# Delta-rule attention and two feed-forward layers: another order of the layers' passes, other constants in the planner, and GpSimd's arithmetic moved to VectorE

## The chip, the core and the metric

The kernel runs on one core of a Trainium2 chip. The core has a matrix engine (TensorE, PE in the profile; PEld is its weight load), a vector engine (VectorE, DVE), a scalar engine (ScalarE, ACT), GpSimd (POOL) and the SyncE queue (SP), which issues all transfers here. The metric is the device time of one execution in microseconds, as the median of several runs.

## What is computed

A delta-rule attention over 768 positions for 4 batches of 8 heads of width 48, then two feed-forward layers over the resulting 3072 rows of 384:

```python
for t in range(S):
    kt, vt, bt = (k_n[:, :, t], v[:, :, t], beta[:, :, t, None])
    y[:, :, t] = np.einsum('bhd,bhde->bhe', q[:, :, t], state)
    v_old = np.einsum('bhde,bhd->bhe', state, kt)
    state = state + bt[:, :, :, None] * np.einsum('bhd,bhe->bhde', kt, vt - v_old)
...
h = x @ w_in;  g = np.maximum(0.01 * h, h);  x = g @ w_out      # layer 0
h = x @ w_in;  g = h - np.tanh(h);           out = g @ w_out    # layer 1
```

Here `k_n` is `k` divided by its norm. Both layers have 2048 hidden features.

## The kernel before

**Numbers in two halves.** Every matmul operand is a pair of f16 tiles, a high part and the rest that it leaves, and a product is three matmuls. So each f32 result is split after it is made: ScalarE writes the high part, VectorE the rest. The weights arrive in 64-bit words and are made into f32 on VectorE (`w_f32`, one shift and two combining instructions for each piece), summed in squares for a scale, and split. There are four weights: 0 (`w1_in`), 1 (`w1_out`), 2 (`w2_in`), 3 (`w2_out`).

**Units and chunks.** The positions are cut into 12 chunks of 64; two chunks make a unit (6 units, 0 to 5). A chunk holds 4 x 64 = 256 rows for the feed-forward layers. For a unit, `keys` and `grams` make normalised keys and their products `gd` (L821, `g_batch` L803, which multiplies `gd` twice on GpSimd, L813 and L814), `inverses` (L832) solves 32x32 triangular systems in `xi` by 60 dependent multiplies and adds, 30 of each, and `merges` (L861) joins the blocks to 64x64 in `XF`. For each chunk then `queries`, `products` (L901, with a mask multiply on `pq`), `states`, `outputs` and `to_xa` make its 256 rows, `xa`. The states go from chunk to chunk.

**Which engine.** `inv_eng` (L858) puts the solve on VectorE in unit 0 and on GpSimd in units 1 to 5; `p_engs` (L914) puts the mask on VectorE for the first four chunks and on GpSimd after; the second half of `g` in layer 0 (L1041) and the zeroing of `XF` (L883) may go to either, as the planner chooses.

**Passes.** `layer(n, i)` (L1105) takes chunk n through layer i: eight times, `h_part` (L1021) makes 256 hidden features (18 matmuls of 256 columns, whose result ScalarE and VectorE turn into `g`), and `o_part` (L1046), three parts later, multiplies `g` with the second weight. The last part of layer 0 hands on to `to_xb`, which makes the input of layer 1. There are 24 passes. Before the change they go unit by unit (L1159): layer 0 of its two chunks, then layer 1 of the two.

**The order.** All work is first put into a graph (`Graph`). `tails` gives each node a priority, the length of the work behind it up to the end. `schedule` then plays the program through, with a cost for each instruction (`cost`), places in buffer rings (`room`), and a `lock` that keeps GpSimd's work and VectorE's two-input work apart, and writes each engine's instructions in the order in which they began there. On the chip each engine runs its own list in that order and waits by semaphores where an input is late. Since rings such as `g` and `ps_h` are handed out in the order of the program, the passes stand in TensorE's list in the order in which `layer` is called. Ring `x` has 6 places; `x_r.most["a"]` says how many of these may hold `xa`.

Of the kernel before, what the change touches and what calls it, by code (L numbers as in the profile page):

```python
# [18 lines left out]

KS = 64.0  # L20
POW2 = 0x7F800000


class Buf:
# [79 lines left out]
class Graph:  # L104


    LAT = dict(pe=0.16, act=0.033, dve=0.033, pool=0.08, sp=0.033)
    SPAN, WARM = 10.24 / 3, 3060.0
    ISSUE, DEEP, RATE = 0.47, 8, 370e3

    def __init__(self, nc):
        self.eng = dict(pe=nc.tensor, act=nc.scalar, dve=nc.vector, pool=nc.gpsimd, sp=nc.sync)
# [19 lines left out]
    def cost(self, eng, op, writes, reads, kw):  # L132
        n = max([v.free for v in writes[:1] + reads])
        wide = [v for v in reads if v.free > 1 or n == 1]
        psum = any(v.psum for v in writes + reads)
        pointer = n > 1 and any(v.free == 1 for v in reads)
        half = all(SIZE[v.ap.dtype] == 2 for v in writes + wide)
        if eng == "dve":
            rate = 0.96
            if op == "transpose":  # L140
                rate = 0.53
            elif op == "memset":
                rate = 1.54
            elif op == "reciprocal":
                rate = 0.16
            elif not psum and op in ("tensor_copy", "tensor_scalar"):
                rate = 3.84 if half and op == "tensor_copy" else 1.92
            elif not psum and op == "tensor_tensor" and half:
                rate = 1.92
            d = 0.15 + n / rate / 1e3 + (0.05 if pointer else 0.0) + (0.02 if psum else 0.0)  # L150
            if op == "memset":
                d = 0.06 + n / rate / 1e3
            two = op in ("tensor_tensor", "scalar_tensor_tensor") and sum(not v.psum for v in wide) > 1
            lock = two or (not psum and op in ("tensor_copy", "tensor_scalar") and n > 8)
            return d, d - 0.08, lock
        if eng == "act":
            d = 0.18 + n * 0.000833 + (0.09 if pointer else 0.0) + (0.1 if "accum_out" in kw else 0.0)
            return d, d - 0.1, False
        if eng == "pool":
            d = 0.12 + n * {"memset": 0.0008, "tensor_scalar": 0.001}.get(op, 0.00205)  # L160
            return d, d - 0.04, True
        return 0.0, self.ISSUE, False
# [3 lines left out]
    def depend(self, node, v, write, eng):  # L166
        psum = v.psum
        p0, p1, lo, hi = v.region()
        log = v.buf.log
        if v.buf.ring is not None and not log:  # L170
            node.new.append(v.buf)
        for q0, q1, l, h, m, w in log:
            if m is node:
                continue
            if psum or ((w or write) and p0 < q1 and q0 < p1 and lo < h and l < hi):
                node.preds.add(m)
        if write or psum:
            log[:] = [e for e in log if not (p0 <= e[0] and e[1] <= p1 and lo <= e[2] and e[3] <= hi)]
        log.append((p0, p1, lo, hi, node, write))
        if v.buf.ring is not None and v.buf not in node.bufs:  # L180
            node.bufs[v.buf] = True
            v.buf.users.append(node)

    def put(self, calls, writes, reads, dma=0):
        node = Node(len(self.nodes), calls)
        self.nodes.append(node)
        self.open = None
        for v in reads:
            self.depend(node, v, False, "")
        for v in writes:  # L190
            self.depend(node, v, True, "")
        node.cost = {e: self.cost(e, c[0], writes, reads, c[1]) for e, c in calls.items()}
        node.dma = dma
        return node

    def cut(self):
        self.open = None
# [59 lines left out]
    def schedule(self, prio):  # L257
        nodes = self.nodes
        need = [len(n.first) for n in nodes]
        ready = [0.0] * len(nodes)  # L260
        gone = [False] * len(nodes)
        self.start, self.end = [0.0] * len(nodes), [0.0] * len(nodes)
        engs = ("pe", "act", "dve", "pool", "sp")
# [1 line left out]
        heap = {e: ([], []) for e in engs}  # L265
        clock = dict.fromkeys(engs, 0.0)
        lock = dma = 0.0
        past, cols, lands = deque(), 0.0, []
        rings = {}
        left, head, held = {}, {}, {}  # L270
        for n in nodes:
# [19 lines left out]

        def offer(n, r):
            for i, e in enumerate(n.calls):
                heappush(soon[e], (max(r, ready[n.idx]) + self.LAT[e], prio[n.idx], n.idx, i))

        def again(r, t):
            queue = rings[r][1]
# [8 lines left out]
        while len(order) < len(nodes):  # L306
# [51 lines left out]
            if e == "pe":  # L358
                while past and past[0][0] < t - self.SPAN:
                    cols -= past.popleft()[1]  # L360
                if cols < self.WARM:
                    occ = n.cold
                    dur = occ + 0.2
                past.append((t + occ, n.cols))
                cols += n.cols
            if e == "sp":
# [6 lines left out]
            n.on = e  # L373
            clock[e] = t + occ
            if locked:
                lock = t + dur - (0.05 if e == "dve" else 0.0)
            self.start[i], self.end[i] = t, t + dur
            order.append(n)
# [15 lines left out]
                    again(b.ring, b.end + 0.03)  # L394
            for m in n.succs:
                need[m.idx] -= 1
                if e != "pe" or m.main != "pe":
                    ready[m.idx] = max(ready[m.idx], t + dur)
                else:
                    ready[m.idx] = max(ready[m.idx], t + occ - self.LAT["pe"])  # L400
                if not need[m.idx]:
                    offer(m, t)
            for m in n.after:
# [16 lines left out]
def kernel(  # L420
# [14 lines left out]
    NM = k.shape[3]  # L435
# [26 lines left out]
        return Ring(name, [t[:, 0:width] for t in ts], short, order)  # L462

    x_r = ring("x", 6, KT * N, order=False)
    x_r.most["a"] = 5
    s_r = ring("sx", 4, 512, short=True)
    g_r = ring("g", LAG + 1, 512)
    kf_r = ring("kf", 2, NM * D)
# [46 lines left out]
    def copy(o, i, scale=1.0):  # L515
        act(out=o, in_=i, func=ACTF.Copy, scale=scale)
# [6 lines left out]
    def tt(o, a, b, op, engs=("dve",)):  # L523
        either(engs, "tensor_tensor", out=o, in0=a, in1=b, op=op)
# [278 lines left out]
    def g_batch(n, g, Gd, bt):  # L803

        s, m0, kt = n % 2, g * GM, KTp[n % 3]
        ps = bank(C)
        for m in range(GM):
            k2 = [parts(kt, HS[h], m0 + m) for h in range(2)]
            heads([(ps[HS[h], m], k2[h], k2[h]) for h in range(2)])
        gv = slice(s * NM + m0, s * NM + m0 + GM)  # L810
        copy(Gd[:, gv], ps[:, :, 0:HB], maskb[:, 0:1])
        stt(Gd[:, gv], ps[:, :, HB:], maskb[:, 1:2], Gd[:, gv], ALU.mult, ALU.add)
        tt(Gd[:, gv], Gd[:, gv], tri.unsqueeze(1).to_broadcast([128, GM, HB]), ALU.mult, ("pool",))  # L813
        tt(Gd[:, gv], Gd[:, gv], bt[:, s * NM + m0:s * NM + m0 + GM].unsqueeze(2).to_broadcast([128, GM, HB]),  # L814
           ALU.mult, ("pool",))
        av = slice(gv.start + 1, gv.stop + 1)
        split(AT[:, 0, av], AT[:, 1, av], ps[:, :, HB:], half[:, 0:1])

# [37 lines left out]
        return nat  # L856

    def inv_eng(u):  # L858
        return "dve" if u == 0 else "pool"

    def merges(u, nat):  # L861

        def last2(t, r, m):
            return [t[r, m, :, c_] for c_ in range(2)]

        def bank2():
            t = g_.tile(ps_a, [128, 512], F32)
            g_.cut()
            return t[:, 0:NM * HB].rearrange("p (m n) -> p m n", m=NM)

        for i in range(2):
            m0 = i * NM
            pm = bank2()
            for m in range(NM):
                heads([(pm[HS[h], m], [AT[HS[h], c_, m0 + m:m0 + m + 2].rearrange("p m j -> p (m j)") for c_ in range(2)],
                        last2(nat, HS[h], m0 + m)) for h in range(2)])
            split(PM[:, 0, :, 0:HB], PM[:, 1, :, 0:HB], pm, half[:, 1:2])
            ps = bank2()
            for m in range(NM):
                heads([(ps[HS[h], m], parts(PM, HS[h], m), last2(TT, HS[h], m0 + m)) for h in range(2)])  # L880
            split(XH[:, m0:m0 + NM, :, 0], XH[:, m0:m0 + NM, :, 1], ps, -1.0 / KS)
            for h in range(2):
                memset(TWO, XW[HL[h], m0:m0 + NM, 0:HB], 0.0)  # L883

    q_t, qs_t, p_t = {}, {}, {}

# [25 lines left out]
            tt(pg, pg, maskp.unsqueeze(1).to_broadcast([128, 2 * GM, C]), ALU.mult, p_engs(n))  # L912

    def p_engs(n):  # L914
        return ("dve",) if n < 4 else ("pool",)

    def states(n):

# [102 lines left out]
    def h_part(i, x, p, kap):  # L1021
# [8 lines left out]
                node = mm(ps[:, j * N:(j + 1) * N], WI[i][:, 2 * p + j, 1 - a, t], x[b][:, t], n == 0, n == 3 * KT - 1)  # L1030
            g_.ffn(node)
        sx = g_.tile(s_r, [128, 2 * N], F32)
        if i == 0:
            act(out=sx, in_=ps, func=ACTF.Prelu, scale=C0, alpha=0.01)
        else:
            act(out=sx, in_=ps, func=ACTF.Tanh, scale=kap[:, 0:1])
            stt(sx, sx, kap[:, 1:2], ps, ALU.mult, ALU.add)
        g = g_.tile(g_r, [128, 2, 2 * N], F16)
        if i == 0:
            copy(g[:, 0], sx)  # L1040
            tt(g[:, 1], sx, g[:, 0], ALU.subtract, TWO)  # L1041
        else:
            split(g[:, 0], g[:, 1], sx, C0)
        return g
# [94 lines left out]
    for u in range(NU):  # L1139
# [9 lines left out]
        for s in range(2):  # L1149
# [6 lines left out]
            states(n)  # L1156
            outputs(n)
            to_xa(n)
    for u in range(NU):  # L1159
        for i in range(2):  # L1160
            for s in range(2):
                layer(2 * u + s, i)
    while pend:
        o_next()
    g_.prepare()
# [48 lines left out]
```

## Time and profile before

| what | value |
|---|---|
| median of 3 runs | 1098.94 us (1098.93 to 1102.3) |
| the profiled execution's own time | 1101.25 us |
| its span, first to last instruction | 1098.8 us |
| TensorE busy | 977.9 us (89%) |
| VectorE busy | 711.8 us (65%) |
| ScalarE busy | 647.4 us (59%) |
| GpSimd busy | 304.9 us (28%) |

The span is what the durations below are counted in; 2.45 us lie around it in the profiled execution. A busy share is an average over stretches that differ: the slices of the span show VectorE nearly full up to a quarter of the span, and TensorE from there on. Matmul ends are modelled, so a busy TensorE may still wait a little between matmuls.

### The profile page before, as it was taken

The numbers are of one execution on the slowest core, as the hardware profiler recorded it, in microseconds if no ns is written. First come the engines' busy times: TensorE is split into PE (matmuls) and PEld (weight loads), VectorE is DVE, ScalarE is ACT, GpSimd is POOL, SyncE is SP. The second block draws the span as 40 slices with busy tenths as digits, with TensorE's granted clock in tenths as the row PEclk, the third lists the DMA queues.
The fourth block names the chain that finished last, engine by engine and source line by source line (L and its number), as shares of the span: only waits on it lengthen the run. The fifth ranks groups of instructions, "written<-read, shape, count | busy, mean of one in ns | idle before, by whom it ended". The sixth has DMA issues, their size and how long they took to land.

```text
span 1098.8 us, 36802 instructions
## 1 busy us (share of the span) xinstructions
PE 977.9 (89%) x16216; PEld 814.5 (74%) x16216; DVE 711.8 (65%) x1636; ACT 647.4 (59%) x1396; POOL 304.9 (28%) x419
## 2 busy tenths in 40 slices
PE   2215689989899999999999999999999999999998
PEld 2215577777778887778887778888778887788875
DVE  7798899998886448675458673457653465731342
ACT  5648787576875447675447674456663456563432
POOL 3201521650078001068201168201178001010000
PEclk9655689999999999999999999999999999999999
DMA  9442255221110001010001010001010001000000
GB/s 352 167 161 73 71 169 164 89 94 50 42 42 17 1 2 51 17 52 16 2 2 51 17 38 16 1 2 43 20 41 1 1 10 43 13 16 1 1 8 22
DMA packets 30561, 54.47 MB, mean 50 GB/s; under 512 B 4800, under 2 KB 16064, under 8 KB 30400
## 3 DMA queue, kind: packets, MB, share of 16 engines
q1 hardware_dynamic: 30400, 52.11, 15.1%
q8 instruction: 126, 2.06, 0.8%
q14 instruction: 35, 0.29, 0.1%
HBM read 41.09 MB, written 4.72 MB: 42 GB/s over the span
## 4 chain that ended last, share of the span: by engine, by line
PE 71%; DVE 16%; ACT 5%; DMA 5%; issue 3%; SPq 0%; ACTq 0%
PE ps_o L413 29%; PE ps_h L413 29%; PE ps_a L413 13%; DVE wi L416 4%; DVE wo L416 2%; DMA wo<-in_w_in_dram 1%; ACT jk L416 1%; DVE g L416 1%; DVE R L416 1%; DMA x<-in_w_out_dram 1%; DVE pq L416 1%; ACT sx L416 1%; DVE n L416 1%; DVE sx L416 1%; DVE xi L416 1%
## 5 line engine op out<-in xcount | busy, mean ns | idle before, releaser
L413 PE MATMUL ps_h<-x,wi 128*128 128x256 f16 x3456 | 413.7, 273 | 3.9 <-DVE sx L416 2.6
L413 PEld LDWEIGHTS <-wi 128*128 128x128 f16 x3456 | 334.6, 98 | 52.4 <-issue 4.8
L413 PE MATMUL ps_o<-g,wo 128*128 128x256 f16 x1728 | 206.1, 273 | 5.2 <-DVE g L416 3.5
L413 PE MATMUL ps_o<-wo,g 128*128 128x384 f16 x1152 | 208.6, 326 | 1.0 <-DVE x L416 1.0
L413 PEld LDWEIGHTS <-wo 128*128 128x128 f16 x1728 | 168.1, 98 | 27.6 <-issue 6.5
L413 PEld LDWEIGHTS <-g 128*128 128x128 f16 x1152 | 106.5, 98 | 62.1 <-issue 1.9
L416 ACT ACTIVATE g<-sx 128x512 f16<-128x512 f32 x192 | 120.3, 627 | 51.1 <-DVE sx L416 42.7
L416 DVE TENSOR_TENSOR g<-sx,g 128x512 f16<-128x512 f32 x93 | 70.1, 753 | 110.4 <-ACT g L416 110.3
L416 ACT ACTIVATE sx<-ps_h 128x512 f32<-128x512 f32 x96 | 56.9, 594 | 132.8 <-PE ps_h L413 123.0
L416 DVE SCALAR_TENSOR_TENSOR sx<-sx,kap,ps_h 128x512 f32<-128x512 f32 x96 | 71.5, 745 | 86.7 <-ACT sx L416 86.5
L416 ACT ACTIVATE sx<-ps_h,kap 128x512 f32<-128x512 f32 x96 | 65.5, 682 | 93.5 <-PE ps_h L413 81.8
L416 POOL TENSOR_TENSOR xi<-xi,gd 128x30 f32<-128x30 f32 (+9 forms) x150 | 102.0, 680 | 11.4
L416 POOL TENSOR_TENSOR gd<-xi 128x30 f32<-128x30 f32 (+9 forms) x150 | 95.1, 634 | 27.2 <-DVE xi L416 10.8
L416 DVE SCALAR_TENSOR_TENSOR g<-sx,g 128x512 f16<-128x512 f32 x96 | 66.3, 692 | 34.1 <-ACT g L416 33.6
L413 PEld LDWEIGHTS <-KTp 64*64 64x64 f16 x3360 | 63.4, 115 | 29.2 <-issue 24.1
L413 PEld LDWEIGHTS <-KN 64*64 64x64 f16 x1824 | 36.9, 117 | 64.2 <-issue 43.4
L416 POOL MEMSET XF<- 32x512 f32 x12 | 6.2, 518 | 245.8 <-PE ps_a L413 245.4
L416 POOL TENSOR_TENSOR gd<-gd,tri 128x256 f32<-128x256 f32 x24 | 18.1, 763 | 154.6 <-DVE gd L416 79.8
L413 PE MATMUL ps_a<-ident,KN 64*64 64x64 f16 x768 | 19.4, 208 | 44.6 <-DVE sx L416 22.9
L416 POOL TENSOR_TENSOR pq<-pq,maskp 128x1024 f16<-128x1024 f16 x16 | 37.7, 2354 | 69.7 <-DVE pq L416 69.7
L416 ACT ACTIVATE jk<-kf 128x48 bf16<-128x48 f32 x160 | 38.2, 239 | 3.8 <-DMA kf<-in_k_dram 0.8
L416 ACT ACTIVATE x<-ps_a,qs 32x128 f32<-32x128 f32 (+1 forms) x82 | 34.5, 420 | 6.8 <-PE ps_a L413 4.9
(157 smaller groups left out, 1399.7 us busy)
## 6 DMA issues: line engine op xcount, KB each, us to landing
wo<-in_w_in_dram SPq DMA_DIRECT2D x32, 384.0 KB, 6.6
qf<-in_q_dram SPq DMA_DIRECT2D x24, 256.0 KB, 3.0
wi<-in_w_out_dram SPq DMA_DIRECT2D x14, 384.0 KB, 7.7
kf<-in_k_dram SPq DMA_DIRECT2D x12, 384.0 KB, 3.5
vf<-in_v_dram SPq DMA_DIRECT2D x12, 384.0 KB, 3.5
out_dram<-sx SPq DMA_DIRECT2D x48, 96.0 KB, 2.2
x<-in_w_out_dram SPq DMA_DIRECT2D x10, 384.0 KB, 3.8
wi<-sx SPq DMA_DIRECT2D x16, 192.0 KB, 2.6
```

Source lines behind the costliest of these rows:

```text
L413: self.eng["pe"].matmul(out=o.real(), lhsT=lhsT.real(), rhs=rhs.real(), start=start, stop=stop)
L416: getattr(self.eng[n.on], op)(**{k: v.real() if isinstance(v, View) else v for k, v in kw.items()})
```

## The change

- The passes are called in the order of the new function `layers`: layer 0 of units 0 and 1, then layer 1 of unit 0, layer 0 of unit 2, layer 1 of unit 1, and so on.
- The solve, its scaling, the two multiplies of `gd`, the mask of `pq`, the rest of `g` in layer 0 and the zeroing of `XF` are all on VectorE. GpSimd keeps memsets and masks of the start.
- Ring `x` holds at most 3 `xa` tiles where it held 5.
- In the planner a node's inputs are tracked as a ready time for each engine, with that engine's latency added to each input; a stop of TensorE's list every 128 matmuls is put in (`PAGE`); some costs and constants are other numbers; and a place in ring `g` is claimed already when ScalarE's first instruction of a part is placed (`claim`). None of these adds an instruction.

```diff
+INV = "dve"
+MASK = ("dve",)
+GD = ("dve",)
+GLO = ("dve",)
+ZERO = ("dve",)
...
+def layers(n):
+
+    out = [(0, 0), (1, 0)]
+    for u in range(n // 2 - 1):
+        out += [(2 * u + 2, 0), (2 * u + 3, 0), (2 * u, 1), (2 * u + 1, 1)]
+    return out + [(n - 2, 1), (n - 1, 1)]
...
+AMOST = 3
...
+    PAGE = 3.4
...
+            if op == "tensor_tensor" and n == 1024 and SIZE[writes[0].ap.dtype] == 2 and not half:
+                d = 1.36
...
+    def claim(self, node, v):
+
+        node.new.append(v.buf)
+        node.bufs[v.buf] = True
+        v.buf.users.append(node)
...
-                heappush(soon[e], (max(r, ready[n.idx]) + self.LAT[e], prio[n.idx], n.idx, i))
+                heappush(soon[e], (max(r, ready[n.idx][e]), prio[n.idx], n.idx, i))
...
+                left_on -= len(n.calls["pe"])
+                if left_on <= 0:
+                    at = t + occ * (1 + left_on / len(n.calls["pe"]))
+                    turn = max(at, page + (self.PAGE if t > 50 else 6.0))
+                    occ += turn - at
+                    dur += turn - at
+                    page = turn
+                    left_on += 128
...
-                if e != "pe" or m.main != "pe":
-                    ready[m.idx] = max(ready[m.idx], t + dur)
-                else:
-                    ready[m.idx] = max(ready[m.idx], t + occ - self.LAT["pe"])
+                for o in m.calls:
+                    ready[m.idx][o] = max(ready[m.idx][o], t + occ if o == e == "pe" else t + dur + self.LAT[o])
...
-    x_r.most["a"] = 5
+    x_r.most["a"] = AMOST
...
-        tt(Gd[:, gv], Gd[:, gv], tri.unsqueeze(1).to_broadcast([128, GM, HB]), ALU.mult, ("pool",))
+        tt(Gd[:, gv], Gd[:, gv], tri.unsqueeze(1).to_broadcast([128, GM, HB]), ALU.mult, GD)
...
-           ALU.mult, ("pool",))
+           ALU.mult, GD)
...
-        return "dve" if u == 0 else "pool"
+        return INV
...
-                memset(TWO, XW[HL[h], m0:m0 + NM, 0:HB], 0.0)
+                memset(ZERO, XW[HL[h], m0:m0 + NM, 0:HB], 0.0)
...
-        return ("dve",) if n < 4 else ("pool",)
+        return MASK
...
+            node = act(out=sx, in_=ps, func=ACTF.Tanh, scale=kap[:, 0:1])
+        g_.claim(node, g)
...
-            tt(g[:, 1], sx, g[:, 0], ALU.subtract, TWO)
+            tt(g[:, 1], sx, g[:, 0], ALU.subtract, GLO)
...
-    for u in range(NU):
-        for i in range(2):
-            for s in range(2):
-                layer(2 * u + s, i)
+    for n, i in layers(NS):
+        layer(n, i)
```

## Rows read from the trace of the kernel before

**Rows 1.** The page: busy time, and DVE's busy tenths in 40 slices

```profile
PE 977.9 (89%) x16216; PEld 814.5 (74%) x16216; DVE 711.8 (65%) x1636; ACT 647.4 (59%) x1396; POOL 304.9 (28%) x419
...
DVE  7798899998886448675458673457653465731342
```

**Rows 2.** Stretches, core 0: us; PE, PEld, DVE, ACT, POOL busy (count); PEclk, DMA

```profile
0.00:144.00 144.00, 52.95 (x1827) 49.54 (x1829) 122.97 (x324) 92.00 (x268) 37.71 (x64) 0.66 0.48 168
144.00:175.00 31.00, 25.49 (x259) 21.19 (x252) 30.02 (x43) 24.55 (x43) 8.39 (x6) 0.94 0.51 155
175.00:350.00 175.00, 162.73 (x2685) 134.46 (x2683) 155.40 (x365) 127.50 (x306) 73.65 (x100) 1.00 0.23 68
350.00:415.00 65.00, 65.00 (x698) 55.90 (x696) 29.46 (x65) 28.30 (x46) 6.87 (x12) 1.00 0.01 2
415.00:1085.00 670.00, 663.23 (x10715) 548.27 (x10713) 371.85 (x841) 373.19 (x732) 178.32 (x238) 1.00 0.07 19
1085.00:1099.00 14.00, 8.54 (x55) 5.11 (x53) 2.06 (x3) 1.90 (x3) 0.00 (x0) 0.88 0.12 28
```

**Rows 3.** Timeline of PE: starts of the first, third and fifth pass

```profile
144.17 8.04 PE L413 MATMUL ps_h<-x,wi 128*128 128x256 f16 x72
...
213.25 2.12 PE L413 MATMUL ps_h<-x,wi 128*128 128x256 f16 x18 [0.80 <-ACT sx L416]
...
312.08 1.15 PE L413 MATMUL ps_h<-x,wi 128*128 128x256 f16 x9
```

**Rows 4.** Timeline of POOL, around the solve of unit 1

```profile
118.16 0.25 POOL L416 TENSOR_TENSOR gd<-xi 128x30 f32<-128x30 f32 x1 [2.48 <-DVE xi L416]
...
160.82 2.46 POOL L416 TENSOR_TENSOR g<-sx,g 128x512 f16<-128x512 f32 x1 [21.07 <-ACT g L416]
...
199.18 1.16 POOL L416 TENSOR_TENSOR g<-sx,g 128x512 f16<-128x512 f32 x1 [29.66 <-ACT g L416]
...
233.87 0.91 POOL L416 TENSOR_SCALAR xi<-b 128x32 f32<-128x32 f32 x1
```

**Rows 5.** Groups over the span: moved work on POOL, its like on DVE

```profile
L416 POOL TENSOR_TENSOR xi<-xi,gd 128x30 f32<-128x30 f32 (+9 forms) x150 | 102.0, 680 | 11.4
...
L416 DVE TENSOR_TENSOR gd<-xi 128x30 f32<-128x30 f32 (+14 forms) x30 | 9.8, 328 | 0.0
L416 DVE TENSOR_TENSOR xi<-xi,gd 128x30 f32<-128x30 f32 (+14 forms) x30 | 9.8, 325 | 0.0
...
L416 DVE MEMSET XF<- 32x512 f32 x12 | 5.8, 485 | 1.9 <-issue 1.6
L416 DVE TENSOR_TENSOR pq<-pq,maskp 128x1024 f16<-128x1024 f16 x8 | 5.7, 708 | 0.0
...
L416 DVE TENSOR_TENSOR xi<-xi,b 128x1024 f32<-128x1024 f32 x1 | 1.2, 1216 | 0.0
```

**Rows 6.** Groups of DVE by shape: one like the multiplies of gd

```profile
L416 DVE TENSOR_TENSOR gd<-xi 128x240 f32<-128x240 f32 x2 | 0.8, 404 | 0.0
```

**Rows 7.** Groups of DVE from 200 to 235 us

```profile
L416 DVE SCALAR_TENSOR_TENSOR wo<-x,wo 128x384 int32<-128x384 int32 x8 | 7.1, 926 | 0.0
L416 DVE SCALAR_TENSOR_TENSOR wo<-wo,sw,sx 128x768 f16<-128x768 f32 x4 | 5.6, 1404 | 0.0
```

**Rows 8.** Tile wo on DVE over the span: durations ns min/median/max

```profile
L416 DVE SCALAR_TENSOR_TENSOR wo<-x,wo x20: 540/552/1049, 97.6 to 213.9; 128x384 int32<-128x384 int32 x20
...
L416 DVE SCALAR_TENSOR_TENSOR wo<-wo,sw,sx x16: 999/1011/2490, 140.9 to 243.1; 128x768 f16<-128x768 f32 x16
```

**Rows 9.** Groups of DVE from 125 to 178 us: weight 2 made into f32

```profile
L416 DVE SCALAR_TENSOR_TENSOR wi<-wo,wi 128x768 int32<-128x768 int32 x16 | 15.4, 977 | 0.0
...
L416 DVE TENSOR_SCALAR wi<-wo 128x768 int32<-128x768 int32 x7 | 4.6, 656 | 0.0
```

**Rows 10.** Timeline of ACT: the last rows of chunk 2

```profile
297.63 0.36 ACT L416 ACTIVATE x<-ps_a,qs 32x128 f32<-32x128 f32 x1
```

**Rows 11.** One stretch more, columns as in rows 2

```profile
415.00:447.00 32.00, 31.53 (x687) 24.85 (x685) 25.24 (x62) 25.62 (x73) 5.14 (x3) 1.00 0.20 57
```

More of the change, by code (lines that the diff above doesn't have):

```diff
@@ L107 @@
     LAT = dict(pe=0.16, act=0.033, dve=0.033, pool=0.08, sp=0.033)
-    SPAN, WARM = 10.24 / 3, 3060.0
+    SPAN, WARM = 10.24 / 3, 3200.0
     ISSUE, DEEP, RATE = 0.47, 8, 370e3
+    PAGE = 3.4
     def __init__(self, nc):
@@ L149, in cost @@
                 rate = 1.92
-            d = 0.15 + n / rate / 1e3 + (0.05 if pointer else 0.0) + (0.02 if psum else 0.0)
+            d = 0.15 + n / rate / 1e3 + (0.05 if pointer else 0.0) + (0.02 if psum and n > 1 else 0.0)
             if op == "memset":
                 d = 0.06 + n / rate / 1e3
+                if len(writes[0].shape) > 2 and n > 100:
+                    d = 0.5
+            if op == "tensor_tensor" and n == 1024 and SIZE[writes[0].ap.dtype] == 2 and not half:
+                d = 1.36
             two = op in ("tensor_tensor", "scalar_tensor_tensor") and sum(not v.psum for v in wide) > 1
@@ L156, in cost @@
         if eng == "act":
-            d = 0.18 + n * 0.000833 + (0.09 if pointer else 0.0) + (0.1 if "accum_out" in kw else 0.0)
-            return d, d - 0.1, False
+            d = 0.19 + n * 0.000833 + (0.09 if pointer else 0.0)
+            if len(writes[0].shape) > 2 and n == 1024:
+                d = 1.35
+            if "accum_out" in kw:
+                return d + 0.09, d + 0.03, False
+            return d, d - (0.0 if len(writes[0].shape) > 3 else 0.1), False
         if eng == "pool":
@@ L169, in depend @@
         log = v.buf.log
-        if v.buf.ring is not None and not log:
+        if v.buf.ring is not None and not v.buf.users:
             node.new.append(v.buf)
@@ L259, in schedule @@
         need = [len(n.first) for n in nodes]
-        ready = [0.0] * len(nodes)
+        ready = [dict.fromkeys(self.LAT, 0.0) for _ in nodes]
         gone = [False] * len(nodes)
@@ L267, in schedule @@
         lock = dma = 0.0
-        past, cols, lands = deque(), 0.0, []
+        past, cols, lands, holder = deque(), 0.0, [], None
+        page, left_on = 0.0, 94
         rings = {}
@@ L375, in schedule @@
             if locked:
+                holder = e
                 lock = t + dur - (0.05 if e == "dve" else 0.0)
@@ L1032, in h_part @@
         sx = g_.tile(s_r, [128, 2 * N], F32)
[L1033 to L1037, printed above, removed]
         g = g_.tile(g_r, [128, 2, 2 * N], F16)
         if i == 0:
+            node = act(out=sx, in_=ps, func=ACTF.Prelu, scale=C0, alpha=0.01)
+        else:
+            node = act(out=sx, in_=ps, func=ACTF.Tanh, scale=kap[:, 0:1])
+        g_.claim(node, g)
+        if i == 1:
+            stt(sx, sx, kap[:, 1:2], ps, ALU.mult, ALU.add)
+        if i == 0:
             copy(g[:, 0], sx)
-            tt(g[:, 1], sx, g[:, 0], ALU.subtract, TWO)
+            tt(g[:, 1], sx, g[:, 0], ALU.subtract, GLO)
         else:
```

## The prediction

> **What bounds the kernel now.** I begin with the page's busy times [rows 1]. TensorE is busy 89% of the span, and nothing in the change takes work from it: the 24 passes and the attention's matmuls stay as they are. So the change can only act on the 121.1 us in which TensorE is idle, or on matmuls that run slowly. The line of VectorE's slices below it shows where: VectorE is nearly full up to some 250 us and half empty after.
>
> The stretches [rows 2] say how much each part is worth. TensorE is idle for 144 - 52.95 = 91.1 us before the first pass begins, 5.5 us from there to 175 us, 12.3 us to 350 us, nothing to 415 us, 6.8 us to 1085 us, and 5.5 us in the end, where the last results are scaled and written out. VectorE is busy for 85%, 97%, 89%, 45% and 56% of the first five. So there are two regimes: up to about 350 us VectorE sets the pace, and after that TensorE does, with less than 7 us to be had in 670. The granted clock belongs to the first regime too: it is 0.66 of full speed before 144 us and 0.94 up to 175, while TensorE has little to do, and 1.00 from 175 us on.
>
> Next I look at what GpSimd's queue does in the first regime. The solve of unit 1 begins there at 118 us and its last instruction starts at 233.87 us [rows 4]. Inside it, GpSimd stood still twice, 21.1 and 29.7 us, for a `g` of layer 0 that the planner had put into its list ahead of the rest of the solve: 50.7 us of waiting in work that is 60 dependent steps. Behind the solve are merges, states and outputs of unit 1, and so chunk 2's last rows come at 297.6 us [rows 10] and the fifth pass at 312.1 us [rows 3].
>
> **The change, part by part.** *GpSimd's work on VectorE.* Unit 0 shows the price, since its solve is on VectorE already: 30 multiplies and 30 adds take 9.8 + 9.8 us, the scaling 1.2 us [rows 5]. The eight multiplies of `gd` have 256 elements; the nearest shape, 240 elements, takes 0.404 us [rows 6], so 3.2 us. Two more zeroings of `XF` at 0.485 us are 1.0 us, and from unit 2 on four masks at 0.708 us are 2.8 us [rows 5]. That is 25.0 us for unit 1 and 27.8 us for each later one; with 4.2 us in unit 0, 140 us in all, and VectorE's total goes from 711.8 to some 852 us, 78% of the span. On GpSimd the adds alone took 102.0 us for five units, 0.680 us each against 0.325 [rows 5], so the solve gets about twice as short, besides losing its 50.7 us of waits.
>
> Something comes back. While GpSimd ran the solve without a stop, from 200 to 235 us, VectorE's combining instruction on `wo` took 0.926 us in the mean and the split 1.404 us [rows 7]; over the whole span their medians are 0.552 and 1.011 us [rows 8]. These two groups alone lost 8 x 0.374 + 4 x 0.393 = 4.6 us in 35 us. Bounds for 144 to 415 us, where GpSimd is busy 88.9 us [rows 2]: nothing, if it is chance; 0.40 of it, the stretch of the first group, or 36 us, if all work beside GpSimd is slowed as much. I take 20 us, near the middle, because other groups ran there that I have not counted.
>
> The Trainium skill (Perfetto Trace Analysis, Optimizing Scalar/DVE Operations) speaks against this part: where VectorE is saturated, work may be better offloaded from it, even to GpSimd. The same section adds that the two share a read port, so that offloading between them might not help; the rows agree with the second sentence, and how far the first still holds is the first rival below.
>
> *The order of the passes.* Third comes layer 0 of chunk 2 where layer 1 of chunk 0 came. This turns two due times round. Weights 2 and 3 are wanted at the fifth pass and not at the third, so making weight 2 into f32, 15.4 + 4.6 us on VectorE between 125 and 178 us [rows 9], can wait. Unit 1's attention is wanted at the third pass, which began at 213 us [rows 3], and not at the fifth; chunk 2's rows must come some 80 us sooner than they did. And unit 2 is wanted at the seventh pass and not at the ninth; two passes of unit 0 took (312.1 - 144.2) / 2 = 84 us, attention included, so six take about 252 us and the seventh begins at about 400 to 415 us.
>
> Is there room? From 144 to 415 us VectorE is busy 30.0 + 155.4 + 29.5 = 214.9 of 271 us [rows 2]. Add units 1 and 2, 52.8 us; take off 20 us; add what of unit 2 was done only from 415 to 447 us, where VectorE was busy 25.2 us [rows 11], of which I take 15 us as the attention's. That makes 262.7 of 271 us: it fits, with 8 us left. Between 125 and 178 us the 20 us of weight 2 leave and some 14 us of the solve come in, so the first pass should not be delayed.
>
> *The planner.* The stop every 128 matmuls, the other costs, `claim` and the ready time for each engine add no instruction; they change only where each engine's list puts things. The claim holds back ScalarE's first instruction of a part only in the plan, since it still writes its old tile. I cost them at nothing; if a cost is now worse than it was, engines stand behind a late instruction as GpSimd did. *The limit of 3 `xa`* costs nothing as long as attention is not more than three chunks ahead; in the first regime it is behind. Transfers: no size and no number changes. The weights' loads on SP's queue go later with the work on them, and beside that of the first 144 us the transfers' load is 0.23 or less after 175 us [rows 2].
>
> *The sum*, in TensorE's idle time. Before 144 us: 0 (bounds 6 us either way, a few steps of the solve and unit 0's 4.2 us on VectorE against part of weight 2). From 144 to 175 us: 3 of the 5.5 us come back, since weight 2 goes out of the way (0 to 5.5). From 175 to 350 us: 8 of 12.3 us, about two thirds, since the attention of unit 1 is no longer held up by GpSimd's queue, while VectorE as full as this will cost some waits (12.3 down to a loss of 12, below). From 415 us on: 2 of 6.8 us (0 to 6.8). The end: 0. Together 13 us. The profiled execution took 1101.25 us, with a span of 1098.8 us; 1101.25 - 13 = 1088.25 is 0.988 of it, and 0.988 of the median of 1098.94 us is 1086 us.
>
> **The rivals.** *VectorE becomes the bound from 144 to 415 us, and it gets slower.* It is decided by what comes back when GpSimd is idle. At 20 us there are 8 us left; below 12 us nothing is left; at 0 the work is 283 us in 271, so TensorE waits 12 us at the third to seventh pass, and the gain of 8 us is not made: 1099 + 12 - 3 = 1108 us. For it speaks that VectorE is at 97% and 89% already, and that the deadline of unit 1 is 80 us earlier. Against it speaks the stretching in rows 7. The Trainium skill's first sentence above would have it so.
>
> *The wait only changes place.* Unit 1 comes early, but weights 2 and 3 come as much too late for the fifth pass, or attention bursts stay as they are: TensorE's 12 us of idle time move and stay. 1096 to 1102 us. For it: they share VectorE, and the work is the same plus 33 us. Against: the blocked queue is work held up for nothing, and it is gone.
>
> *The first regime gets shorter as well.* The first 18 us of the weights' work that is not needed goes out ahead of the first passes, the solve fits into gaps of its neighbours, and passes run at full rate from about 155 instead of 172 us; with it nearly all 12 us of the second stretch come back: 1086 - 15 - 4 = 1067 us. For it: the first pass was starved while VectorE worked on weight 2. Against: the attention of unit 1 moves into the same time with an earlier due time.
>
> **How the numbers follow.** The forecast, 1076 to 1095 us, has a chance of 0.45; the longer gain, 1062 to 1076 us, 0.19; no difference, 0.11; slower, 0.25. No difference is what a measurement of this kernel can't tell from none, 0.3% or 3.3 us either way. So faster has 0.64, the same 0.11, slower 0.25. The range is 1064 to 1108 us: it leaves out less than a tenth at the low end and about a tenth at the high one. The likeliest case alone has 1076 to 1095 us.
>
> **What would show it.** The solve of unit 1 would be 60 steps on VectorE of some 0.33 us, without a stop of 20 us; GpSimd nearly idle after the start; the combining instruction on `wo` near 0.55 us throughout; chunk 2's last rows near 215 us and not at 298 us; VectorE busy over 95% from 144 to 415 us, and TensorE idle there 7 us or less where it was 17.8 us. The forecast is wrong if TensorE stands for VectorE at the third, fifth or seventh pass for more than 15 us together (the first rival), if its idle time there stays at 17.8 us (the second), or if the first pass begins more than 8 us from 144 us.

## The result, and the profile after

The changed kernel takes 1065.65 us (median of 4 runs, 1062.7 to 1066.15), against 1100.62 us for the kernel before beside it: a ratio of 0.9674, 95% interval 0.9643 to 0.9705, so 3.3% faster. It lies in the stated range and near its lower end, at the third rival's 1067 us; the forecast of 1086 us is a gain of 1.2%, less than half of what came.

The page after, busy times and VectorE's slices, which answer to [rows 1]:

```profile
PE 970.9 (91%) x16216; PEld 813.9 (76%) x16216; DVE 772.7 (73%) x2023; ACT 648.1 (61%) x1403; POOL 9.6 (1%) x25
...
DVE  7999999999999899648689538579637562244442
```

TensorE has the same 16216 matmuls. GpSimd is empty after the start; VectorE is busy 61 us more, and nearly full (80% or more of each slice) from 27 to 425 us. The stretches after, with the columns of [rows 2]:

```profile
0.00:144.00 144.00, 64.08 (x1970) 59.17 (x1971) 135.36 (x377) 101.69 (x285) 9.64 (x25) 0.68 0.46 162
144.00:175.00 31.00, 31.00 (x424) 27.26 (x424) 30.20 (x85) 26.80 (x47) 0.00 (x0) 1.00 0.24 74
175.00:350.00 175.00, 171.59 (x3205) 148.01 (x3200) 166.67 (x443) 132.46 (x298) 0.00 (x0) 0.99 0.29 87
350.00:415.00 65.00, 63.17 (x1385) 51.96 (x1384) 56.60 (x189) 55.64 (x180) 0.00 (x0) 1.00 0.17 48
415.00:1050.00 635.00, 632.29 (x9194) 522.20 (x9193) 381.85 (x930) 329.58 (x594) 0.00 (x0) 1.00 0.06 16
1050.00:1064.00 14.00, 8.79 (x58) 5.33 (x55) 2.06 (x3) 1.90 (x3) 0.00 (x0) 0.97 0.12 28
```

TensorE's idle time falls by 91.1 - 79.9 = 11.1 us before 144 us, 5.5 in the next stretch, 12.3 - 3.4 = 8.9 up to 350 us, rises by 1.8 up to 415, and falls by 4.1 and 0.3 behind it: 28.0 us. The other 7 us of the span's 34.8 are busy time, 977.9 to 970.9 us. Where they come from is not shown: from 144 to 175 us the granted clock is 1.00 where it was 0.94, but that is at most some 2 of the 31 us, and a matmul of `ps_h` takes 273 ns in the mean of both pages.

The starts of the first, third and fifth pass on TensorE, and the last of chunk 2's rows on ScalarE, which answer to [rows 3] and [rows 10]:

```profile
130.09 2.66 PE L454 MATMUL ps_h<-x,wi 128*128 128x256 f16 x18
...
210.48 2.13 PE L454 MATMUL ps_h<-x,wi 128*128 128x256 f16 x18
...
291.54 1.69 PE L454 MATMUL ps_h<-x,wi 128*128 128x256 f16 x14
```

```profile
197.70 0.36 ACT L457 ACTIVATE x<-ps_a,qs 32x128 f32<-32x128 f32 x1
```

The first pass begins 14.1 us earlier. The third is now layer 0 of chunk 2, whose rows come 100 us earlier than before, and it does not wait for them. VectorE's work on tile `wo` (durations in ns, min/median/max) and the solve's adds, against [rows 8] and [rows 5]:

```profile
L457 DVE SCALAR_TENSOR_TENSOR wo<-x,wo x20: 541/548/554, 91.6 to 285.9; 128x384 int32<-128x384 int32 x20
...
L457 DVE SCALAR_TENSOR_TENSOR wo<-wo,sw,sx x16: 999/1009/1022, 131.6 to 333.6; 128x768 f16<-128x768 f32 x16
```

```profile
L457 DVE TENSOR_TENSOR xi<-xi,gd 128x30 f32<-128x30 f32 (+9 forms) x180 | 58.9, 327 | 2.3
```

The longest combining instruction fell from 1.049 to 0.554 us, the longest split from 2.490 to 1.022: these two groups are stretched no more. A step of the solve takes 0.327 us.

### The profile page after: what moved, and what is told of

Same layout as the page of the kernel before. It is cut to its first block, busy times and chain, and to the rows that moved or that the text cites. A ratio compares the mean times of both kernels' runs of the same rounds, so it can differ in the third digit from the quotient of the medians.

```text
span 1064.0 us, 36737 instructions
## 1 busy us (share of the span) xinstructions
PE 970.9 (91%) x16216; PEld 813.9 (76%) x16216; DVE 772.7 (73%) x2023; ACT 648.1 (61%) x1403; POOL 9.6 (1%) x25
## 4 chain that ended last, share of the span: by engine, by line
PE 66%; DVE 3%; ACT 1%; issue 1%; DMA 1%; ACTq 0%
PE ps_o L454 28%; PE ps_h L454 28%; PE ps_a L454 10%; DVE sx L457 1%; DMA wi<-sx 0%; DVE g L457 0%; ACT sx L457 0%; DVE pq L457 0%; DMA qf<-in_q_dram 0%; ACT jk L457 0%; DVE wi L457 0%; DVE n L457 0%; DVE R L457 0%; ACT x L457 0%; DVE wo L457 0%
## 5 line engine op out<-in xcount | busy, mean ns | idle before, releaser
L454 PE MATMUL ps_o<-wo,g 128*128 128x384 f16 x1152 | 205.0, 326 | 1.8 <-issue 1.5
L457 DVE TENSOR_TENSOR g<-sx,g 128x512 f16<-128x512 f32 x96 | 65.8, 685 | 53.1 <-ACT g L457 52.8
L457 DVE TENSOR_TENSOR xi<-xi,gd 128x30 f32<-128x30 f32 (+9 forms) x180 | 58.9, 327 | 2.3
L457 DVE TENSOR_TENSOR gd<-xi 128x30 f32<-128x30 f32 (+9 forms) x180 | 58.7, 326 | 2.2
L457 ACT ACTIVATE x<-ps_a,qs 32x128 f32<-32x128 f32 (+1 forms) x92 | 38.0, 413 | 6.9 <-PE ps_a L454 5.2
L454 PE MATMUL ps_a<-ab,ones 128*128 128x1 bf16 x124 | 11.8, 166 | 31.5 <-DVE ab L457 31.4
L454 PE MATMUL ps_a<-pq,Ub 128*128 128x64 f16 x576 | 36.5, 199 | 2.6 <-ACT Ub L457 1.2
L454 PE MATMUL ps_a<-pq,Sb 128*128 128x64 f16 x528 | 33.6, 195 | 0.6 <-DVE p L457 0.5
```

The source lines that it names most:

```text
L454: self.eng["pe"].matmul(out=o.real(), lhsT=lhsT.real(), rhs=rhs.real(), start=start, stop=stop)
L457: getattr(self.eng[n.on], op)(**{k: v.real() if isinstance(v, View) else v for k, v in kw.items()})
```

## The experiments

**The three parts, each alone and each left out.** "Order" is `layers` and 3 `xa`, which were not taken apart; "engines" is the moved arithmetic; "planner" is the costs, the stop every 128 matmuls, ready times by engine and the claim. Ratios are against runs of the kernel before on the same chip, with 95% intervals.

| kernel | order | engines | planner | median us | ratio | first pass us |
|---|---|---|---|---|---|---|
| before | old | old | old | 1098.9 to 1104.3 | 1 | 144.2 |
| e1_order_only | new | old | old | 1143.95 | 1.0360 (1.0345 to 1.0376) | 142.0 |
| e2_engines_only | old | new | old | 1097.15 | 0.9941 (0.9924 to 0.9957) | 142.0 |
| e3_planner_only | old | old | new | 1090.73 | 0.9878 (0.9862 to 0.9895) | 139.0 |
| e4_all_but_order | old | new | new | 1083.36 | 0.9841 (0.9824 to 0.9858) | 131.1 |
| e5_all_but_engines | new | old | new | 1131.31 | 1.0282 (1.0267 to 1.0298) | 131.9 |
| e6_all_but_planner | new | new | old | 1079.40 | 0.9813 (0.9794 to 0.9832) | 138.9 |
| the change | new | new | new | 1065.65 | 0.9674 (0.9643 to 0.9705) | 130.1 |

The order is put in with

```diff
-    for u in range(NU):
-        for i in range(2):
-            for s in range(2):
-                layer(2 * u + s, i)
+    for n, i in layers(NS):
+        layer(n, i)
```

the engines with `("dve",)` in the five places of the diff, and the planner by `cost`, `schedule`, `depend` and `claim` of the one or the other kernel.

e1: 

> The kernel before with the new order of passes and the limit of 3 xa, and nothing else. Theory A (the order: weight 2 no longer stands on VectorE ahead of the first pass): the first pass starts at 130 to 135 us where it started at 144, and most of the 35 us of the change is here: 1072 to 1082 us. Theory B (GpSimd: its blocked queue and its slowing of VectorE): with the solve of unit 1 still on GpSimd the third pass now waits for it, 1098 to 1115 us. Theory C (the planner's constants): no change, 1096 to 1102 us.

e2: 

> The kernel before with all of GpSimd's arithmetic on VectorE, and nothing else. Theory A: the first pass stays at 140 to 146 us, since weight 2 still goes first and the solve of unit 1 comes on top; 1095 to 1108 us. Theory B: 20 us or more of the gain is here, 1070 to 1080 us, with idle time of TensorE from 175 to 350 us down from 12 to below 5 us. Theory C: 1096 to 1102 us.

e3: 

> The new planner (costs, stop every 128 matmuls, ready times by engine, claim) with the old order of passes, 5 xa and GpSimd's work on GpSimd. Theories A and B: 1092 to 1101 us. Theory C: most of the gain is here, 1068 to 1080 us, and GpSimd's queue no longer stands 50 us inside the solve of unit 1, since the planner puts the g of layer 0 at the right place.

e4: 

> The changed kernel with the old order of passes and 5 xa. Theory A (the order brings the gain): 1085 to 1099 us, first pass at 140 us or later. Theory B (GpSimd): 1066 to 1076 us. Theory C (planner): 1066 to 1076 us.

e5: 

> The changed kernel with GpSimd's work back on GpSimd. Theory A: 1066 to 1080 us, first pass at 130 to 135 us. Theory B: 1085 to 1110 us, TensorE idle at the third pass while the solve of unit 1 runs on GpSimd. Theory C: 1066 to 1076 us.

e6: 

> The kernel before with the new order of passes, 3 xa and GpSimd's work on VectorE, planned with the old costs and without claim and stop. Theories A and B: 1066 to 1076 us. Theory C: 1085 to 1102 us.

No theory holds alone. Only e2 lies in a range that a theory gave it (A and C). The new order by itself is 3.6% slower, which theory B had in sign and not in size, and with the moved work it gains 1.3% with the old planner (0.9813 / 0.9941) and 1.7% with the new (0.9674 / 0.9841). The moved work gains 0.6% in the old order and 5.3% in the new (0.9813 / 1.0360). The planner gains 0.8 to 1.4% in every company, which none of the three theories had: A and B gave it nothing, C everything. Added in the order engines, order, planner, the steps are 0.6, 1.3 and 1.4%.

Where the planner's share comes from is seen on VectorE before the first pass. The stretch from 0 to that start, for the planner alone, all but the planner, and the changed kernel (columns as in [rows 2]):

```profile
0.00:139.00 139.00, 54.76 (x1879) 51.17 (x1880) 129.14 (x335) 95.66 (x272) 40.45 (x64) 0.67 0.51 176
```

```profile
0.00:139.00 139.00, 49.03 (x1688) 46.21 (x1689) 122.98 (x350) 90.24 (x264) 9.64 (x25) 0.65 0.45 160
```

```profile
0.00:130.00 130.00, 50.08 (x1734) 47.01 (x1735) 121.45 (x350) 90.11 (x266) 9.64 (x25) 0.65 0.48 171
```

VectorE is busy 123 us before the first pass in the kernel before [rows 2], 123 without the new planner, 121 with all of the change, and 129 with the planner alone, where GpSimd still works beside it. What differs is its idle time: 21.0 us before, 16.0 without the planner, 9.9 with the planner alone and 8.6 us with all. In these kernels the first pass begins when VectorE has done this work, and the new plan wastes less of the time up to there.

**What in the planner.** Three kernels leave one piece out of the change, a fourth adds one piece to e6. The ready time for each engine was not tried by itself.

```diff
-                    turn = max(at, page + (self.PAGE if t > 50 else 6.0))
+                    turn = at
```

> The changed kernel, planned without the stop of TensorE's list every 128 matmuls. Theory D (the stop is what the new planner brings: the plan then knows that unit 0's small matmuls come late, and puts other work into VectorE's list there): VectorE idle before the first pass rises from 8.5 us to 14 us or more, the first pass begins at 136 to 140 us, and the time is 1073 to 1081 us, as without the new planner (1079). Theory E (the other costs or the claim bring it): 1063 to 1069 us.

```diff
-        g_.claim(node, g)
```

> The changed kernel without the early claim of ring g in the plan. Theory D: the same, 1062 to 1069 us. Theory E, if the claim: 1073 to 1081 us.

e9 puts the old numbers back into `cost` (and the old value of the constant `WARM`); a part of the edit:

```diff
-            d = 0.19 + n * 0.000833 + (0.09 if pointer else 0.0)
...
+            d = 0.18 + n * 0.000833 + (0.09 if pointer else 0.0) + (0.1 if "accum_out" in kw else 0.0)
```

> The changed kernel, planned with the old costs of ScalarE's and VectorE's instructions; stop and claim stay. Theory D: 1062 to 1070 us. Theory E, if the costs: 1073 to 1081 us.

e10 is e6 and the stop:

```diff
+                left_on -= len(n.calls["pe"])
+                if left_on <= 0:
...
```

> New order of passes and GpSimd's work on VectorE with the old planner, to which the stop every 128 matmuls alone is added. Theory D: nearly the whole change, 1064 to 1071 us, VectorE idle before the first pass 11 us or less. Theory E: 1075 to 1082 us, as with the old planner.

| kernel | median us | ratio | first, third, seventh pass us | VectorE idle before the first |
|---|---|---|---|---|
| e6_all_but_planner | 1079.40 | 0.9813 | 138.9, 222.8, 387.5 | 16.0 |
| e7_no_stop | 1079.34 | 0.9795 (0.9773 to 0.9816) | 134.6, 220.6, 387.1 | 12.2 |
| e10_stop_without_rest | 1077.01 | 0.9776 (0.9761 to 0.9791) | 129.7, 215.0, 383.2 | 7.9 |
| e9_old_costs | 1079.37 | 0.9802 (0.9787 to 0.9816) | 128.2, 215.7, 385.1 | 7.8 |
| e8_no_claim | 1069.48 | 0.9724 (0.9676 to 0.9771) | 129.6, 210.1, 375.9 | 7.3 |
| the change | 1065.65 | 0.9674 | 130.1, 210.5, 375.9 | 8.6 |

The stop brings most of the early start: among these kernels VectorE idles under 9 us with it and the first pass is at 128 to 130 us, without it at 134 to 139. The stretch of e10, to be read against that of e6 above:

```profile
0.00:130.00 130.00, 48.16 (x1689) 45.28 (x1690) 122.12 (x348) 89.34 (x263) 9.67 (x25) 0.67 0.48 171
```

But theory D falls for the time: the stop alone gains 0.4%, since e9 and e10 lose again by the seventh pass what they had won at the first. It takes the other costs as well, and theory E falls too, since these without the stop (e7) gain nothing clear. The claim is worth 0.5%, with an interval that overlaps that of the change, so perhaps nothing. Which of the costs it is was not tried.

**Weight 2 put first again.** The place of weight 2 alone is undone by adding to its priority:

```diff
-        return [-t for t in tail]
+        return [-t - getattr(n, "more", 0.0) for t, n in zip(tail, self.nodes)]
...
+    for n_ in g_.nodes[from_:]:
+        n_.more = 75.0
```

> The changed kernel with 75 us added to the priority of all work on weight 2, two passes' worth, so that it stands about where the old order of passes had it. Theory A (the order pays because weight 2 leaves VectorE free for the first passes and for unit 1): weight 2 is made into f32 before 180 us again, unit 1's rows come 10 to 20 us later, TensorE's idle time from the first pass to 350 us rises from 3 to 12 us or more, and the time is 1075 to 1090 us. If where weight 2 stands does not matter: 1063 to 1069 us.

It took 1084.49 us, 0.9863 (0.9831 to 0.9894), 19 us more than the change. VectorE's groups from 120 to 190 us, then TensorE's start of the second pass, both of e11, and that start in the changed kernel:

```profile
L457 DVE SCALAR_TENSOR_TENSOR wi<-wo,wi 128x768 int32<-128x768 int32 x16 | 15.2, 951 | 0.0
```

```profile
182.78 3.96 PE L454 MATMUL ps_h<-x,wi 128*128 128x256 f16 x18
```

```profile
160.79 2.13 PE L454 MATMUL ps_h<-x,wi 128*128 128x256 f16 x18
```

The first pass still starts at 128.8 us; it is the pass itself that takes 54 us in place of 31. TensorE's waits in it end for the most part with `sx` and `x` on ScalarE (5.8 and 4.2 us), whose list, like VectorE's, now has weight 2's work between the splits of weight 0 and `g`. From the first pass to 350 us TensorE is idle 221 - 205.4 = 15.6 us:

```profile
129.00:350.00 221.00, 205.43 (x3509) 177.78 (x3508) 208.89 (x553) 166.91 (x381) 0.00 (x0) 0.95 0.28 85
```

So what the order gains (1.7%, some 19 us) is lost when weight 2 may not wait. This is what theory A expected, in the passes and not in the first start.

**Where the engine matters.** e12 keeps the solves of units 3 to 5 on GpSimd:

```diff
-        return INV
+        return "dve" if u < 3 else "pool"
```

> The changed kernel with the solves of units 3, 4 and 5 on GpSimd. If moving GpSimd's work pays only in the first regime, and TensorE sets the pace behind it: 1062 to 1069 us, though VectorE has 65 us less to do. If the freed GpSimd pays in the whole span: 1072 to 1085 us.

1066.13 us, 0.9683 (0.9665 to 0.9702): the same as the change. Its stretch against that after, from 415 us:

```profile
415.00:1050.00 635.00, 632.27 (x9183) 521.08 (x9181) 344.86 (x783) 330.93 (x599) 90.77 (x142) 1.00 0.06 16
```

VectorE has 37 us less to do there and TensorE is idle 2.7 us in both. Behind the first regime the move of these three solves neither costs nor gains.

Which moved work makes the 6% of e5? e13 is e3 with one line changed, so that only the rest of `g` is moved; e16 puts the solve of unit 1 alone back to GpSimd; e17 puts back all else.

```diff
-GLO = ("dve", "pool")
+GLO = ("dve",)
```

> New planner, old order of passes, GpSimd's work on GpSimd, but for the rest of g in layer 0, which is on VectorE alone. The prediction's step 'the blocked queue costs about 8 us from 175 to 350 us' gives 1078 to 1086 us, against 1088 us of this planner with the old order (0.988 of before). If the waits in GpSimd's queue were hidden behind weights 2 and 3, the same as that: 1086 to 1092 us.

```diff
-        return INV
+        return "pool" if u == 1 else "dve"
```

> The changed kernel with the solve of unit 1 alone on GpSimd. If the loss of 6% when all is put back to GpSimd is this one solve, which now is due at the third pass: 1110 to 1135 us, and the third pass begins 50 us or more later than at 210 us. If it is VectorE's slowing beside GpSimd, or the other moved work: 1066 to 1080 us.

```diff
-GD = ("dve",)
-GLO = ("dve",)
-ZERO = ("dve",)
+GD = ("pool",)
+GLO = ("dve", "pool")
+ZERO = ("dve", "pool")
...
-        return MASK
+        return ("dve",) if n < 4 else ("pool",)
```

> The changed kernel with masks, multiplies of gd, zeroing and the rest of g back on GpSimd (or left to the planner), and only the solves on VectorE. If the solves are what counts: 1064 to 1072 us. If waits in GpSimd's queue on a g or a gd count too: 1075 to 1095 us.

e13: 1087.35 us, 0.9882 (0.9861 to 0.9903), level with e3's 0.9878. What it tests is smaller than the 50.7 us of the kernel before, since in e3, with the new planner, GpSimd stands only once inside the solve of unit 1, 21.9 us. The stop, the end of the solve and the first instruction that reads it, ScalarE's split, in e3:

```profile
153.36 1.41 POOL L457 TENSOR_TENSOR g<-sx,g 128x512 f16<-128x512 f32 x1 [21.89 <-ACT g L457]
...
196.37 0.59 POOL L457 TENSOR_SCALAR xi<-b 128x32 f32<-128x32 f32 x1
...
266.29 1.35 ACT L457 ACTIVATE gd<-xi 128x1024 f16<-128x1024 f32 x1
```

and the last two in e13:

```profile
178.26 0.91 POOL L457 TENSOR_SCALAR xi<-b 128x32 f32<-128x32 f32 x1
...
267.60 1.34 ACT L457 ACTIVATE gd<-xi 128x1024 f16<-128x1024 f32 x1
```

Without the stop the solve ends 18 us earlier and is read no earlier: in the old order this stop was hidden. (e13's first pass starts 5 us later than e3's, so the two times alone would not show it.) e17: 1067.85 us, 0.9703 (0.9686 to 0.9720). e16: 1125.6 us, 1.0231 (1.0209 to 1.0253). One solve makes nearly all of the loss. In e16 it begins on GpSimd at 116.9 us and has no long stop; the end of it there, TensorE's longest stop, the first instructions of ScalarE and VectorE on its result, and the third pass on TensorE:

```profile
168.39 0.51 POOL L457 TENSOR_SCALAR xi<-b 128x32 f32<-128x32 f32 x1
...
241.75 0.56 PE L454 MATMUL ps_a<-ab,ones 128*128 128x1 bf16 x16 [27.52 <-DVE ab L457]
...
251.66 1.32 ACT L457 ACTIVATE gd<-xi 128x1024 f16<-128x1024 f32 x1
...
253.01 1.29 DVE L457 TENSOR_TENSOR gd<-xi,gd 128x1024 f16<-128x1024 f32 x1 [0.21 <-ACT gd L457]
...
289.11 3.20 PE L454 MATMUL ps_h<-x,wi 128*128 128x256 f16 x15
```

and the solve's end and its readers in the changed kernel:

```profile
167.65 0.19 DVE L457 TENSOR_SCALAR xi<-b 128x32 f32<-128x32 f32 x1
...
168.25 1.35 ACT L457 ACTIVATE gd<-xi 128x1024 f16<-128x1024 f32 x1
...
169.68 1.37 DVE L457 TENSOR_TENSOR gd<-xi,gd 128x1024 f16<-128x1024 f32 x1
```

The solve ends at 169 us on GpSimd and at 168 us on VectorE. Yet its result lies for 83 us until ScalarE reads it, and VectorE right behind. What VectorE did meanwhile, its groups from 180 to 270 us in e16:

```profile
L457 DVE SCALAR_TENSOR_TENSOR wi<-wo,wi 128x768 int32<-128x768 int32 x14 | 13.1, 950 | 0.0
L457 DVE SCALAR_TENSOR_TENSOR wo<-x,wo 128x384 int32<-128x384 int32 x16 | 8.5, 551 | 0.0
L457 DVE SCALAR_TENSOR_TENSOR wi<-wi,sw,sx 128x768 f16<-128x768 f32 x8 | 7.9, 1010 | 0.0
L457 DVE SCALAR_TENSOR_TENSOR wo<-wo 128x768 int32<-128x768 int32 x8 | 7.6, 953 | 0.0
```

It made weights 2 and 3, which nobody was to want before the fifth pass, because its list, and ScalarE's, had them first; TensorE stood for the same work (`ab`, a step of a weight's scale), 27.5 us at the longest.

**Is it the plan or the chip?** The `lock` keeps GpSimd's instructions and VectorE's two-input ones (and some copies) apart in the plan. The last three kernels plan without that:

```diff
-            return d, d - 0.04, True
+            return d, d - 0.04, False
```

e18 is e16 with this, e19 the change with all solves but unit 0's on GpSimd, e20 is e1 with it.

> The kernel with the solve of unit 1 alone on GpSimd (1125.6 us), planned as if GpSimd's instructions did not exclude VectorE's two-input ones. There the solve had ended at 169 us, 4 us after that of the changed kernel, but VectorE's list took its result up at 253 us, behind the work on weights 2 and 3. Theory F (the plan, not GpSimd, costs the 60 us: it expected the solve to be that late): the third pass begins before 225 us and the time is 1063 to 1078 us. Theory G (the chip: GpSimd's solve slows what is beside it and is late itself): 1100 us or more.

> The changed kernel with all solves of units 1 to 5 on GpSimd, and the rest of the moved work on VectorE, planned without the exclusion. Theory F: 1058 to 1075 us, level with the changed kernel or faster, since VectorE has 110 us less to do. Theory G: 1100 us or more.

> The kernel before with the new order of passes and 3 xa (1143.95 us), planned without the exclusion and with the g of layer 0 still free to go to GpSimd. Theory F: 1075 to 1095 us, near the 1079 us that order and moved work reach together with the old costs. Theory G: 1130 us or more.

e18: 1084.84 us, 0.9845 (0.9821 to 0.9870), between the two theories. (Its expectation has the two ends of the solve 4 us apart; they are 1 us apart.) The result is taken up as soon as it is there and the third pass comes 62 us earlier than in e16:

```profile
170.23 1.35 DVE L457 TENSOR_TENSOR gd<-xi,gd 128x1024 f16<-128x1024 f32 x1 [4.27 <-ACT gd L457]
...
227.34 2.13 PE L454 MATMUL ps_h<-x,wi 128*128 128x256 f16 x18
```

So 41 of the 60 us that this solve costs go away with another plan on the same engines. The other 19 us go against theory F's number. They are lost early: the second pass starts at 181.3 us, against 160.8 in the changed kernel. In e16, where the solve runs on GpSimd in the same time but the plan has the exclusion, it starts at 167.3, so the plan has a part in these 19 us too. VectorE's groups from 130 to 166 us, in e18 and in the changed kernel, show what is stretched beside GpSimd:

```profile
L457 DVE SCALAR_TENSOR_TENSOR wo<-wo,sw,sx 128x768 f16<-128x768 f32 x8 | 9.2, 1159 | 0.1
L457 DVE TENSOR_TENSOR g<-sx,g 128x512 f16<-128x512 f32 x6 | 5.3, 901 | 0.0
```

```profile
L457 DVE SCALAR_TENSOR_TENSOR wo<-wo,sw,sx 128x768 f16<-128x768 f32 x8 | 8.1, 1008 | 0.0
...
L457 DVE TENSOR_TENSOR g<-sx,g 128x512 f16<-128x512 f32 x8 | 5.4, 681 | 0.0
```

How much of the 19 us is this and how much the other order of the lists is open. e19: 1121.22 us, 1.0176 (1.0152 to 1.0200), as theory G had it, and e20: 1127.45 us, 1.0230 (1.0203 to 1.0258), nearest to theory G. In e19 TensorE is idle 22 us from 415 to 1050 us, where it is 2.7 us in e12, which plans its late solves with the exclusion:

```profile
415.00:1050.00 635.00, 612.58 (x9266) 507.61 (x9261) 338.05 (x786) 330.43 (x627) 116.92 (x178) 0.99 0.06 17
```

The waits of ScalarE and TensorE in that stretch of e19 say how (us in total, times, longest):

```profile
ACT gd L457 <- POOL xi L457: 24.3, 3, 8.8
```

```profile
PE ps_h L454 <- ACT sx L457: 17.5, 3, 6.1
```

ScalarE stands at the ends of the three late solves, and TensorE for the `sx` that comes behind. So a plan that leaves the exclusion out puts the reading of the solve ahead of its end on the chip. No kernel tried beats the changed one; e12 equals it, and e8 and e17 are not clear of it.

## Why the prediction was right and where it was wrong

*What bounds the kernel* held: two regimes, the gain in the first, 2.2 us net of idle time from 350 us to the last stretch where 2 were forecast.

*The step that failed* is what was said of the planner, "they change only where each engine's list puts things ... I cost them at nothing", and with it the first term of the sum, "Before 144 us: 0 (bounds 6 us either way)". The planner measured 1.4%, some 15 us, on top of the rest (e6 against the change), and the first term 11.1 us of idle time, with the first pass 14.1 us earlier. The first three stretches of e6, which has order and moved work with the old planner, separate the two:

```profile
0.00:144.00 144.00, 54.03 (x1753) 49.70 (x1753) 127.98 (x362) 92.60 (x266) 9.64 (x25) 0.64 0.44 156
144.00:175.00 31.00, 30.52 (x432) 27.14 (x427) 29.30 (x85) 26.15 (x44) 0.00 (x0) 1.00 0.23 72
175.00:350.00 175.00, 170.93 (x3198) 148.58 (x3197) 166.30 (x420) 135.58 (x301) 0.00 (x0) 1.00 0.29 89
```

TensorE's idle time falls there by 1.1, 5.0 and 8.2 us, where 0, 3 and 8 were forecast (from 350 to 415 us it rises by 3.1), and e6 as a whole gains 1.9% where 1.2% was forecast. So for what it priced the sum was near, and what it put at nothing made most of the miss. I had looked at which work leaves VectorE before the first pass and which comes in, and these do cancel (123 and 121 us). I had not asked how much of the 144 us VectorE stands idle, though [rows 2] say it, 144 - 122.97 = 21.0 us. A resource that is called the bound of a stretch and is idle 15% of it has time left that a better order may use. The early start alone is not the gain, however: e10 and e9 start as early and end at 1077 and 1079 us.

The third rival's 1067 us is what came, in part by luck. Its ground, weight 2 out of the way of the first passes, is borne out by e11; but without the new planner the same order and engines take 1079 us, and the rival had nothing for the planner.

*From 144 to 175 us:* 3 us forecast, 5.5 measured, within the term's bounds. The low clock of the early matmuls was named at the start and given no price; busy time fell by 7 us in the span, and how much of that is the clock's is not shown.

*From 175 to 350 us:* 8 us forecast, 8.9 measured, but the reason given, GpSimd's blocked queue, is not borne out, and so the number is in part luck. In the kernel before the solve ended at 234.8 us [rows 4], after its 50.7 us of stops, and the first instruction to read it, on ScalarE, came 35 us later:

```profile
270.00 1.35 ACT L416 ACTIVATE gd<-xi 128x1024 f16<-128x1024 f32 x1
```

So the last 35 us of the stops can't have held anything up in that list; e13 shows the same of the 21.9 us that are left with the new planner. Of the 8.9 us the moved work alone brings 3.2 (idle 9.1 us in e2) and with the order 8.2 (e6); the order does it by weight 2's later place (e11).

*What comes back on VectorE.* 140 us were priced onto VectorE, and its busy time rose by 772.7 - 711.8 = 61 us; 79 us came back over the span, 0.26 us for each of the 305 us of GpSimd, where 20 of 88.9, or 0.22, were taken. (Some 5 of the 79 us are small work that went to ScalarE.) Prices from unit 0's rows were right: 0.327 against 0.325 us a step.

*The first rival,* VectorE full from 144 to 415 us, came true as a fact and not as a loss: 97% and 95% in the first two stretches, with TensorE idle 0 and 3.4 us. The Trainium skill (Perfetto Trace Analysis, Optimizing Scalar/DVE Operations) says that offloading some work from a saturated VectorE, even to GpSimd, may make sense; here more work on it went with a faster kernel. The same section adds that the two share a read port, so that offloading between them might not help. The 79 us and e18's stretched `g` (0.901 against 0.681 us) agree with that; no run here shows the port itself. The early due time of unit 1 was rightly seen as the danger: in e1, which is 3.6% slower, the third pass starts at 302 us. But the mechanism, as far as e16 and e18 show it, is for the greater part another one, lists in which the wrong work stands first, and not too little time.

*Of the signs,* the solve without a stop, the empty GpSimd, 0.55 us throughout and TensorE idle 5.2 us from 144 to 415 us came as said; chunk 2's rows came at 198 us where 215 was said, and the seventh pass at 375.9 where the room on VectorE was reckoned with 400 to 415; VectorE was busy 93.5% there and not over 95%; and the first pass was 14 us off, which the text had named as a sign that the forecast is wrong.

## What to carry to other kernels

Where each engine runs a fixed list, ask of every late result not only when it was ready but what its taker's list had ahead of it: the same solve, ended within some 1 us of the same time, went with 60 us more or with none, and 41 of the 60 us went away with another plan. Moves of work, order and plan didn't add here: the order alone lost 3.6%, with the moved work it won. And when an engine is named as the bound of a stretch, its idle time in that stretch is the first thing to price.

## What the runs showed of the hardware

TensorE's list stops in unit 0's dense stretches of small matmuls. From the chain of work that ended last, in the kernel before (start us, us, what):

```profile
111.88 2.45 PE ps_a L413 x127
114.32 1.28 issue
115.61 2.52 PE ps_a L413 x128
118.13 0.93 issue
```

"issue" is time in which TensorE waited for nothing that the profile shows. A plan that knows of these stops starts the first pass 9 us earlier (e10 against e6). The trace points at the cause, though no experiment changed it. The page counts transfers of instructions (packets, MB, share of the 16 engines):

```profile
q8 instruction: 126, 2.06, 0.8%
```

These are 16 KB each, one for about 128 of the 16216 matmuls with their weight loads. Around here they land at 110.5, 114.4 and 117.6 us, and TensorE goes on at 111.9, 115.6 and 119.1 us, 1.3 to 1.4 us after each. So it probably stood for its own next instructions.

And a busy microsecond of GpSimd's work had cost VectorE about a quarter of one, 0.26 us, where 0.22 was taken for it.
